# Hashed attention and a squared-ReLU block: another way of loading and transposing the first pair of heads

## The chip, the cores and the metric

The kernel runs on one core of a Trainium2 chip. The metric is the device time of one execution in microseconds, as the median of several runs. The engines named here are TensorE (PE in the profile, with its weight loads as PEld), VectorE (DVE), ScalarE (ACT), GpSimd (POOL) and SyncE (SP), which issues DMAs. ACT and POOL issue DMAs as well.

## The reference

Attention in which a query sees only the keys with the same six-bit hash, then a two-layer block with a squared ReLU.

```python
# q, k, v: (4, 8, 768, 64), proj: (64, 6)
q_bits = (np.einsum('bhsd,dk->bhsk', q, proj) > 0).astype(np.int64)
k_bits = (np.einsum('bhsd,dk->bhsk', k, proj) > 0).astype(np.int64)
powers = 2 ** np.arange(n_bits)
q_bucket = np.sum(q_bits * powers, axis=-1)
k_bucket = np.sum(k_bits * powers, axis=-1)
mask = q_bucket[:, :, :, None] == k_bucket[:, :, None, :]
scores = np.where(mask, scale * np.matmul(q, k.transpose(0, 1, 3, 2)), -1000000000.0)
scores = scores - np.max(scores, axis=-1, keepdims=True)
attn = np.exp(scores)
attn = attn / (np.sum(attn, axis=-1, keepdims=True) + 1e-09)
attn_out = np.matmul(attn, v)
x = attn_out.transpose(0, 2, 1, 3).reshape(3072, 512)
h = x @ w_in                       # (512, 2048)
r = np.maximum(h, 0.0)
out = (r * r) @ w_out              # (2048, 512)
```

## The kernel before

**The whole.** The attention part takes the 32 heads as 16 pairs, two heads of 64 features on the 128 partitions, and lasts to about 318 us. The rest of the span is the two-layer block, done in chunks of 1024 tokens with fewer block products than the plain scheme (`product`, line 828, and `hidden_pair`, line 1091). The order of all instructions is written out by hand under `tc.manual_schedule()` (line 656): each engine runs its own instructions in that order and waits where an operand or a buffer is not ready.

**One pair.** The features of queries and keys stand as `feat`, [features of two heads, query or key, 768 tokens]. The scores come in blocks of 128 keys by 384 queries by two heads (`score`, line 439): `products` multiplies bf16 marks of the hash bits (`bits`), whose product is zero for equal hashes and hugely negative otherwise, and adds the fp32 products of the features in the same PSUM buffer. The first block of the first pair (`first_score`, line 448) has them the other way round: first the feature products of both query halves, then the mark products of both. ACT takes the exponential (`weight`, line 434) into a ring of four `e` tiles. `attend` multiplies `e` by the values, and DVE sums the `e` tiles (`add_up`).

**The marks.** `hash_bits` multiplies the projection by `feat`. For pairs 1 to 15, ACT makes signs of it, and POOL's DMAs place them (`signs`, `weigh`, `place_bits`). The first pair goes another way: `first_signs` (line 364) makes the query marks on ACT in four instructions, and `first_keys` (line 400) the key marks of one half c of the keys on DVE, two comparisons (line 409) and one scaling (line 413).

**PSUM.** There are three pools: `turn` has two buffers that all score blocks, hashes and transposed halves take in turn, `spare` has one, and `xo` has one, called `void` ahead of the first pair and taken by the sums over the values (`outs`) later. Each is of two banks.

**The first pair.** `load_first` (line 277) loads queries and keys: for each of the two and for each head one DMA, head 0 on SP's queue, head 1 on ACT's. A partition holds, for each of six blocks t of 128 tokens, the token t * 128 + p: runs of 64 floats, 256 bytes. Then the projection is loaded for both heads. `keep_busy` (line 333) issues products of ones that nobody reads. `first_features(w, r)` (line 314) transposes three blocks of two heads at once, for the queries (w = 0) or the keys (w = 1) and the first or second half of the tokens (r), into a `turn` buffer. ACT copies the queries to `feat`, DVE the keys (lines 326 and 328). With four such halves and two buffers, the third waits for the copy of the first, the fourth for that of the second, and the two buffers of `first_score` for the copies of the two key halves. All later pairs come by `load_pair` (line 291), eight DMAs on SP's queue in runs of 128 bytes, and are transposed by DVE (`features`, line 340).

**The order at the start** (lines 657 to 674): the ones and zeros, the loads of the first pair, eight filler products, the identity on POOL, constants on DVE and POOL, the loads of pair 1, of the first values (`load_values`, line 305) and of two weight pieces, the query halves, two filler products, the first key half, the hash of the queries into `void`, their signs, the hash of the first keys into `spare` and their marks, the second key half. Then, in the loop over pairs, `load_pair(2)`, `first_score` and `first_keys(1, spare("hash"))`, before the other blocks.

Of the kernel before, what the change touches and what calls it, by code (L numbers as in the profile page):

```python
# [8 lines left out]
FP32 = mybir.dt.float32  # L9
BF16 = mybir.dt.bfloat16  # L10
# [24 lines left out]
def kernel(  # L35
# [10 lines left out]
    nc = tc.nc  # L46
    PSUM = bass.MemoryType.PSUM

    B, H, S, D = q.shape
# [3 lines left out]
    P = 128  # L53
    SB = S // P
    HS = S // 2
# [15 lines left out]
    ident = glob.tile([P, P], FP32, name="ident")  # L71
# [19 lines left out]
    p_qk = first.enter_context(tc.tile_pool(name="p_qk", bufs=2))  # L91
# [4 lines left out]
    const = first.enter_context(tc.tile_pool(name="const", bufs=1))  # L96
# [7 lines left out]
    def turn(name):  # L104

        return ps_s.tile([P, 2, 512], FP32, name=name, tag="turn")

    def spare(name):

        return ps_t.tile([P, 2, 512], FP32, name=name, tag="spare")  # L110
# [164 lines left out]
    nat, feat, bits = {}, {}, {}  # L275

    def load_first():

        both = p_qk.tile([P, 2, SB, 2, D], FP32, name="qk_nat")
        for w, src in enumerate((q, k)):  # L280
            t = both[:, w]
            for h, queue in enumerate((nc.sync, nc.scalar)):
                queue.dma_start(
                    out=t[:, :, h], in_=src[0, h].rearrange("(t p) d -> p t d", t=SB)
                )
        nat[0, "qk"] = both
        feat[0] = p_f.tile([P, 2, S], FP32, name="feat")
        for h, queue in enumerate((nc.sync, nc.scalar)):
            queue.dma_start(out=projs[h * D:(h + 1) * D, 0:NBITS], in_=proj)
# [15 lines left out]
    def load_values(pr):  # L305
        b, j = divmod(pr, PB)
        t = p_v.tile([P, 2, SB * D], FP32, name="v_nat")
        nc.sync.dma_start(
            out=t.rearrange("p h (t d) -> p (h t) d", d=D),
            in_=v[b, 2 * j:2 * j + 2].rearrange("h (t p) d -> p (h t) d", t=SB),  # L310
        )
        nat[pr, "v_nat"] = t

    def first_features(w, r):

        tp = turn("tp")[:, 0]
        for i in range(SB // 2):
            t = r * (SB // 2) + i
            nc.tensor.transpose(  # L319
                out=tp[:, i * P:(i + 1) * P],  # L320
                in_=nat[0, "qk"][:, w, t].rearrange("p h d -> p (h d)"),
                identity=ident,
            )
        out = feat[0][:, w, r * HS:(r + 1) * HS]
        if w == 0:
            nc.scalar.copy(out=out, in_=tp[:, 0:HS])
        else:
            nc.vector.tensor_copy(out=out, in_=tp[:, 0:HS])  # L328

    busy = const.tile([P, 512], BF16, name="busy")  # L330
    void = ps_o.tile([P, 2, 512], FP32, name="xo")

    def keep_busy(n, w=512):

        for _ in range(n):
            nc.tensor.matmul(
                out=void[:, 0, 0:w], lhsT=busy[:, 0:P], rhs=busy[:, 0:w], start=True, stop=True
            )

    def features(pr):  # L340
# [9 lines left out]
    def hash_bits(pr, banks, ws=(0, 1), cs=(0, 1)):  # L350


        for w in ws:
            hashed[pr, w] = banks
            for c in cs:
                g = 2 * w + c
                for h in range(2):
                    rows = slice(h * D, (h + 1) * D)
                    nc.tensor.matmul(  # L359
                        out=banks[g * NR_B:(g + 1) * NR_B, h, 0:HS], lhsT=projs[rows],  # L360
                        rhs=feat[pr][rows, w, c * HS:(c + 1) * HS], start=True, stop=True,
                    )

    def first_signs(w):

        bits[0, w] = t = all_bits[0][:, w]
        for c in range(2):
            at = slice((2 * w + c) * NR_B, (2 * w + c + 1) * NR_B)
            for h in range(2):
                nc.scalar.activation(  # L370
                    out=t[h * D:h * D + NR_B, c * HS:(c + 1) * HS], in_=hashed[0, w][at, h, 0:HS],
                    func=ACTF.Sign, scale=HUGE, bias=lifts[at],
                )
# [26 lines left out]
    def first_keys(c, banks):  # L400

        if c == 0:
            bits[0, 1] = all_bits[0][:, 1]
        t = bits[0, 1]
        hash_bits(0, banks, (1,), (c,))
        at = slice((2 + c) * NR_B, (3 + c) * NR_B)
        cut = slice(c * HS, (c + 1) * HS)
        for h in range(2):
            nc.vector.tensor_scalar(  # L409
                out=t[h * D:h * D + NR_B, cut], in0=banks[at, h, 0:HS],  # L410
                scalar1=0.0, scalar2=None, op0=ALU.is_gt,
            )
        nc.vector.tensor_scalar(
            out=t[:, cut], in0=t[:, cut], scalar1=spans, scalar2=bases, op0=ALU.mult,
            op1=ALU.add,
        )
# [204 lines left out]
    for pr in range(NIN, NP):  # L621
        n = 16 if pr == NP - 1 else 1 + (pr % 3 == 0)
# [13 lines left out]
    def order(n):  # L636

        s = n % NR
        return s if n < NR else s % 2 * NQ + s // 2
# [14 lines left out]
        minus(*((t1, b12, b11), (t2, b22, t1), (t3, b22, b12), (b12, b21, t2))[n - 1])  # L654

    with tc.manual_schedule():
        nc.vector.memset(busy, 1.0)
        nc.vector.memset(projs, 0.0)
        load_first()
        keep_busy(8)  # L660
        make_identity(nc, ident)
        constants()
        load_pair(1)
        load_values(0)
        for i in range(2):
            load_weight(i)
        first_features(0, 0)
        first_features(0, 1)
        keep_busy(2)
        first_features(1, 0)  # L670
        hash_bits(0, void, (0,))
        first_signs(0)
        first_keys(0, spare("hash"))
        first_features(1, 1)


# [1 line left out]
        for pr in range(NP):  # L678
# [86 lines left out]
            if more:  # L765
                load_values(pr + 1)
# [28 lines left out]
        pr = NP - 1  # L795
# [626 lines left out]
        for i in range(NCHUNK):  # L1422
            for s in range(NR):
                r = order(i * NR + s)
# [245 lines left out]
```

## Time and profile before

| What | us |
|---|---|
| median of 3 runs | 858.05 (857.92 to 859.75) |
| the profiled execution | 858.97 |
| its span | 857.2 |
| TensorE busy up to 12.51 us | 8.95 |
| TensorE busy from 12.51 to 857.20 | 839.20 |
| DVE busy up to 12.51, from there | 4.17, 745.11 |
| ACT busy up to 12.51, from there | 4.43, 397.60 |

The span is the stretch that the profiler records; the time of the execution is 1.8 us longer. At 12.51 us the first mark products of the first pair begin (line 429, `st` from `bits`). Busy times of matmuls have modelled ends, so neighbouring ones overlap, and a busy TensorE need not be at its peak. In the chain of waits, each step is followed back to what released it.

### The profile page before, as it was taken

Reading aid. Unit: us, or ns where it says so; the run is one execution under the profiler, and the core shown is the slowest. Engines: PE = TensorE matmul, PEld = TensorE weight load, DVE = VectorE, ACT = ScalarE, POOL = GpSimd, SP = SyncE. Lnnn points to the kernel's source line nnn. Section 1 sums busy time; section 2 is a strip of 40 time slices with the busy share of each in tenths; the row PEclk is TensorE's granted clock in tenths of the full one; section 3 lists DMA queues with packets and bytes.
Section 4 is the critical chain, followed back from the end, with each engine's and each line's share of the span. In section 5 each row is a group of like instructions: output and inputs, shape, how many; then the busy total and the mean of one; then the engine's idle time right before and its main releaser. Section 6 shows DMA issues by size and latency. Waiting matters only on the chain.

```text
span 857.2 us, 16996 instructions
## 1 busy us (share of the span) xinstructions
PE 848.1 (99%) x6593; PEld 529.0 (62%) x6593; DVE 749.3 (87%) x1026; ACT 402.0 (47%) x752; POOL 166.6 (19%) x280
## 2 busy tenths in 40 slices
PE   8999999999999999999999999999999999999997
PEld 3544444444444544444788875657888765668886
DVE  5899999999999988998879978888889788889776
ACT  5887777788877762222211145554111355541110
POOL 1221111113321101653122121111000311100002
PEclk9999999999999999999999999999999999999999
DMA  9676899889998525999976976437557865335466
GB/s 204 133 143 153 176 183 196 201 161 260 247 227 227 169 69 215 342 308 296 355 235 227 264 184 218 163 114 277 196 153 195 179 239 176 124 120 154 149 168 140
DMA packets 236132, 170.12 MB, mean 198 GB/s; under 512 B 169576, under 2 KB 193200, under 8 KB 236048
## 3 DMA queue, kind: packets, MB, share of 16 engines
q1 hardware_dynamic: 195376, 87.85, 41.4%
q0 software_dynamic: 16480, 42.41, 15.9%
q10 hardware_dynamic: 24192, 38.74, 14.7%
q8 instruction: 53, 0.87, 0.4%
q14 instruction: 31, 0.25, 0.1%
HBM read 127.14 MB, written 41.16 MB: 196 GB/s over the span
## 4 chain that ended last, share of the span: by engine, by line
PE 97%; DMA 1%; DVE 0%; POOL 0%; ACT 0%; issue 0%; ACTq 0%; DVEq 0%
PE acc L837 41%; PE st L429 18%; PE xo L484 14%; PE acc L1099 13%; PE acc L1052 8%; PE tot L533 2%; PE hash L359 1%; DMA qk_nat<-in_k_dram 1%; DMA bits<-signed 1%; POOL bits L395 0%; DVE bits L409 0%; PE xo L359 0%; ACT e L435 0%; DVE feat L328 0%; PE tp L319 0%
## 5 line engine op out<-in xcount | busy, mean ns | idle before, releaser
L435 ACT ACTIVATE e<-st 128x768 f32<-128x768 f32 x192 | 155.4, 810 | 59.2 <-PE st L429 56.2
L429 PE MATMUL st<-feat 64*64 64x384 f32 x1536 | 158.0, 483 | 1.0 <-DVE feat L328 1.0
L484 PE MATMUL xo<-e,v_nat 64*64 64x385 f32 (+1 forms) x1520 | 157.6, 483 | 0.0
L837 PE MATMUL acc<-b,leaf 128*128 128x256 f32 x600 | 133.3, 379 | 0.4 <-issue 0.4
L837 PEld LDWEIGHTS acc<-b,leaf 128*128 128x128 f32 x600 | 113.8, 190 | 16.8 <-issue 1.3
L472 DVE TENSOR_TENSOR total<-total,e 128x1536 f32<-128x1536 f32 x64 | 111.8, 1746 | 4.3 <-ACT e L435 2.8
L395 POOL DMA_DIRECT2D bits<-signed x120 | 61.9, 520 | 217.2 <-ACT signed L384 198.4
L484 PEld LDWEIGHTS xo<-e,v_nat 64*64 64x64 f32 (+1 forms) x1520 | 57.3, 133 | 66.4 <-issue 57.8
L1099 PE MATMUL acc<-t_x,w_unit 128*128 128x512 f32 x192 | 90.9, 595 | 0.0
L429 PEld LDWEIGHTS st<-feat 64*64 64x64 f32 x1536 | 56.3, 133 | 38.7 <-issue 33.3
L837 PE MATMUL acc<-t,leaf 128*128 128x256 f32 x336 | 76.0, 379 | 0.0
L837 PEld LDWEIGHTS acc<-t,leaf 128*128 128x128 f32 x336 | 63.8, 190 | 8.7
L914 DVE SCALAR_TENSOR_TENSOR b<-h 128x512 f32<-128x512 f32 x96 | 65.7, 691 | 3.0
L429 PE MATMUL st<-bits 64*64 64x384 bf16 x768 | 65.9, 325 | 0.3
L837 PE MATMUL acc<-x,w_unit 128*128 128x512 f32 x128 | 56.5, 593 | 0.0
L837 PE MATMUL acc<-b_t,leaf 128*128 128x256 f32 x240 | 53.8, 379 | 0.0
L844 ACT COPY two<-acc 128x256 f32<-128x256 f32 (+1 forms) x29 | 12.5, 432 | 87.5 <-PE acc L837 72.1
L1099 PEld LDWEIGHTS acc<-t_x,w_unit 128*128 128x128 f32 x192 | 35.8, 190 | 26.7 <-issue 23.0
L1220 POOL DMA_DIRECT2D out_dram<-h x24 | 15.5, 654 | 182.1 <-DVE h L1215 182.1
L844 ACT COPY one<-acc 128x256 f32<-128x256 f32 (+1 forms) x29 | 12.5, 432 | 78.8 <-PE acc L837 63.7
L837 PEld LDWEIGHTS acc<-b_t,leaf 128*128 128x128 f32 x240 | 45.6, 190 | 6.2
L429 PEld LDWEIGHTS <-bits 64*64 64x64 bf16 x768 | 24.2, 107 | 38.1 <-issue 37.5
(178 smaller groups left out, 1287.9 us busy)
## 6 DMA issues: line engine op xcount, KB each, us to landing
leaf<-w_out ACTq DMA_DIRECT2D x142, 256.0 KB, 3.0
raw<-in_moe_w_in_dram SPq DMA_DIRECT2D x8, 1024.0 KB, 6.7
raw<-in_moe_w_out_dram SPq DMA_DIRECT2D x8, 1024.0 KB, 7.9
w_unit<-w_in SPq DMA_DIRECT2D x16, 512.0 KB, 4.0
w_unit<-w_in SPq DMA_DIRECT2D x8, 896.0 KB, 8.4
w_out<-sums POOLq DMA_DIRECT2D x16, 448.0 KB, 7.6
v_nat<-in_v_dram SPq DMA_DIRECT2D x16, 384.0 KB, 5.2
x_all<-x_t SPq DMA_DIRECT2D x16, 384.0 KB, 3.2
```

The lines of the kernel that those rows point to most:

```text
L395: nc.gpsimd.dma_start(out=t[h * D:h * D + NBITS + 1, w, c * HS:(c + 1) * HS], in_=signed[at:at + NBITS + 1, h],)
L429: nc.tensor.matmul(out=st[k * HK:(k + 1) * HK, h, 0:HS], lhsT=src[1][rows, key], rhs=src[0][rows, cut], start=first, stop=not first, skip_ ...
L435: nc.scalar.activation(out=key_of(pr, kt)[:, :, i, 0:HS], in_=st[:, :, 0:HS], func=ACTF.Exp, scale=scale)
L472: nc.vector.tensor_tensor(out=totals[pr], in0=totals[pr], in1=e, op=ALU.add)
L484: return nc.tensor.matmul(out=outs[pr][h * D:(h + 1) * D, c, 0:HS + 1], lhsT=nat[pr, "v_nat"][rows, h, kt * D:(kt + 1) * D], rhs=key_of(pr ...
L533: done = nc.tensor.matmul(out=spares[pr][g * 32:(g + 1) * 32, c2, 0:QS], lhsT=ones[rows], rhs=totals[pr][rows, h, c, c2 * QS:(c2 + 1) * QS ...
L837: nc.tensor.matmul(out=acc[to], lhsT=a(i), rhs=b(i), start=first and i == 0, stop=last and i == n - 1, skip_group_check=True,)
L844: nc.scalar.copy(out=t, in_=acc[of])
L914: nc.vector.scalar_tensor_tensor(out=out, in0=h, scalar=0.0, in1=h, op0=ALU.max, op1=ALU.mult)
L1052: nc.tensor.matmul(out=out, lhsT=w(a), rhs=b, start=start, stop=stop, skip_group_check=True)
L1099: nc.tensor.matmul(out=to, lhsT=w[:, PLACE[a], f], rhs=bt[b](f), start=first and f == 0, stop=last and f == NFT // 2 - 1, skip_group_check ...
L1220: queue.dma_start(out=out[at, m0 + a * 32:m0 + (a + 1) * 32].rearrange("(c i) j -> i c j", i=32), in_=ot[a * 32:(a + 1) * 32].rearrange("i ...
```

## The change

It touches the first pair alone.

- `load_first`: a partition now holds six consecutive tokens of each head, p * 6 + t, so a run is 384 floats, 1536 bytes. The tile is [partition, query or key, head, t, feature].
- `first_features`: for each block t, one product per head of the loaded [128 tokens, 64 features] with the identity, an ordinary fp32 matmul, instead of one transpose of both heads. The column x of block t is then token x * 6 + t. For the queries, ACT's copy writes every sixth element and so restores the order of the tokens. For the keys, DVE's copy leaves the order as it is. The second key half goes into the `spare` buffer, the others into `turn`.
- `load_values`: the first pair's values are loaded in the same order as the keys, six consecutive tokens to a partition, in runs of 1536 bytes.
- The hash of the first keys goes into `void`. That of the later keys stays in `spare`.
- `keep_busy`: six filler products instead of eight, and the two after the query halves are gone. Their ones are a tile of 128 columns that is read four times over, filled by POOL instead of DVE.

```diff
@@ -276,12 +276,12 @@
 
     def load_first():
 
-        both = p_qk.tile([P, 2, SB, 2, D], FP32, name="qk_nat")
+        both = p_qk.tile([P, 2, 2, SB, D], FP32, name="qk_nat")
         for w, src in enumerate((q, k)):
-            t = both[:, w]
             for h, queue in enumerate((nc.sync, nc.scalar)):
                 queue.dma_start(
-                    out=t[:, :, h], in_=src[0, h].rearrange("(t p) d -> p t d", t=SB)
+                    out=both[:, w, h].rearrange("p t d -> p (t d)"),
+                    in_=src[0, h].rearrange("(p t) d -> p (t d)", t=SB),
                 )
         nat[0, "qk"] = both
         feat[0] = p_f.tile([P, 2, S], FP32, name="feat")
@@ -305,36 +305,44 @@
     def load_values(pr):
         b, j = divmod(pr, PB)
         t = p_v.tile([P, 2, SB * D], FP32, name="v_nat")
-        nc.sync.dma_start(
-            out=t.rearrange("p h (t d) -> p (h t) d", d=D),
-            in_=v[b, 2 * j:2 * j + 2].rearrange("h (t p) d -> p (h t) d", t=SB),
-        )
+        vs = v[b, 2 * j:2 * j + 2]
+        if pr == 0:
+            nc.sync.dma_start(out=t, in_=vs.rearrange("h (p t) d -> p h (t d)", t=SB))
+        else:
+            nc.sync.dma_start(
+                out=t.rearrange("p h (t d) -> p (h t) d", d=D),
+                in_=vs.rearrange("h (t p) d -> p (h t) d", t=SB),
+            )
         nat[pr, "v_nat"] = t
 
     def first_features(w, r):
 
-        tp = turn("tp")[:, 0]
+        tp = (spare("tp") if (w, r) == (1, 1) else turn("tp"))[:, 0]
+        ts = slice(r * (SB // 2), (r + 1) * (SB // 2))
         for i in range(SB // 2):
-            t = r * (SB // 2) + i
-            nc.tensor.transpose(
-                out=tp[:, i * P:(i + 1) * P],
-                in_=nat[0, "qk"][:, w, t].rearrange("p h d -> p (h d)"),
-                identity=ident,
+            for h in range(2):
+                nc.tensor.matmul(
+                    out=tp[h * D:(h + 1) * D, i * P:(i + 1) * P],
+                    lhsT=nat[0, "qk"][:, w, h, ts.start + i], rhs=ident, start=True, stop=True,
+                )
+        if w == 0:
+            nc.scalar.copy(
+                out=feat[0][:, w].rearrange("p (x t) -> p t x", t=SB)[:, ts],
+                in_=tp[:, 0:HS].rearrange("p (t x) -> p t x", x=P),
             )
-        out = feat[0][:, w, r * HS:(r + 1) * HS]
-        if w == 0:
-            nc.scalar.copy(out=out, in_=tp[:, 0:HS])
         else:
-            nc.vector.tensor_copy(out=out, in_=tp[:, 0:HS])
-
-    busy = const.tile([P, 512], BF16, name="busy")
+            nc.vector.tensor_copy(out=feat[0][:, w, r * HS:(r + 1) * HS], in_=tp[:, 0:HS])
+
+    busy = const.tile([P, P], BF16, name="busy")
     void = ps_o.tile([P, 2, 512], FP32, name="xo")
 
-    def keep_busy(n, w=512):
-
+    def keep_busy(n):
+
+        wide = busy.rearrange("p (o n) -> p o n", o=1).to_broadcast([P, 4, P])
         for _ in range(n):
             nc.tensor.matmul(
-                out=void[:, 0, 0:w], lhsT=busy[:, 0:P], rhs=busy[:, 0:w], start=True, stop=True
+                out=void[:, 0].rearrange("p (o n) -> p o n", o=4), lhsT=busy, rhs=wide,
+                start=True, stop=True,
             )
 
     def features(pr):
@@ -654,10 +662,10 @@
         minus(*((t1, b12, b11), (t2, b22, t1), (t3, b22, b12), (b12, b21, t2))[n - 1])
 
     with tc.manual_schedule():
-        nc.vector.memset(busy, 1.0)
+        nc.gpsimd.memset(busy, 1.0)
         nc.vector.memset(projs, 0.0)
         load_first()
-        keep_busy(8)
+        keep_busy(6)
         make_identity(nc, ident)
         constants()
         load_pair(1)
@@ -666,11 +674,10 @@
             load_weight(i)
         first_features(0, 0)
         first_features(0, 1)
-        keep_busy(2)
         first_features(1, 0)
         hash_bits(0, void, (0,))
         first_signs(0)
-        first_keys(0, spare("hash"))
+        first_keys(0, void)
         first_features(1, 1)
```

## The prediction

> **What bounds the kernel now.** I read the page first. TensorE is busy for 99% of the span, and its granted clock is 9 tenths or more in all 40 slices.
>
> ```profile
> PE 848.1 (99%) x6593; PEld 529.0 (62%) x6593; DVE 749.3 (87%) x1026; ACT 402.0 (47%) x752; POOL 166.6 (19%) x280
> PEclk9999999999999999999999999999999999999999
> ```
>
> So 857.2 - 848.1 = 9.1 us of TensorE idleness is in the whole span, and an edit that removes no needed product gains only by starting the dense stream sooner. Busy time split at 12.51 us shows 8.95 us of TensorE work before that point, 3.6 of the idle 9.1 us, and much of the 8.95 is filler (L336). After it DVE is busy 745.1 of 844.7 us and TensorE 839.2, so TensorE stays the pace. The next view is the chain of waits of the first 45 us (start, length, what).
>
> ```profile
> 1.51 5.90 DMA qk_nat<-in_k_dram
> 7.50 0.52 PE tp L319 x3
> 8.02 0.86 PE xo L359 x8
> 8.88 0.65 PE hash L359 x4
> 9.63 0.55 DVE bits L409
> 10.20 0.57 DVE bits L409
> 10.79 0.38 DVE bits L413
> 11.20 0.57 DVE feat L328
> 11.81 1.20 PE st L429 x16
> ```
>
> The reader sees one serial thread: the keys of head 1 land at 7.41, are transposed, the queries and then the first keys are hashed, DVE makes the key marks, and only then copies the second half of the keys out of PSUM (L328, 11.20 to 11.77). TensorE stands until that copy, because the second score buffer is the one being copied. The score stream's mark products begin at 12.51, and from there TensorE hardly stops. I use 12.51 as the mark to be moved. The timeline from 0 to 12 us shows what is ahead.
>
> ```profile
> 1.69 3.60 PE L336 MATMUL xo<-busy 128*128 128x512 bf16 x8 [1.69 <-DVE excess L255]
> 2.09 0.15 PEld L336 LDWEIGHTS <-busy 128*128 128x128 bf16 x1 [0.28 <-issue]
> 2.52 0.15 PEld L336 LDWEIGHTS <-busy 128*128 128x128 bf16 x1 [0.28 <-issue]
> 5.18 1.04 PE L319 MATMUL tp<-ident,qk_nat 128*128 128x128 f32 x6
> 8.99 2.36 ACT L370 ACTIVATE bits<-xo,lifts 32x384 bf16<-32x384 f32 x4 [2.21 <-issue]
> ```
>
> Filler products are 0.43 us apart (512 columns), about half the speed of the later stream, where 256 columns in two-pass fp32 take 0.222 us (L837: 133.3 us / 600). The first transpose took 448 ns, the others 272. So the array speeds up at about 5.2 us, which the granted clock does not show.
>
> The DMA view from 0 to 3 us gives the landings (last number, us after issue began): q at 0.97 + 3.6 = 4.6 and 0.98 + 4.1 = 5.1, k at 1.48 + 4.8 = 6.3 and 7.4, the projection at 7.8 and 8.0.
>
> ```profile
> qk_nat<-in_q_dram SPq DMA_DIRECT2D x1, 192.0 KB, 3.6
> qk_nat<-in_q_dram ACTq DMA_DIRECT2D x1, 192.0 KB, 4.1
> qk_nat<-in_k_dram SPq DMA_DIRECT2D x1, 192.0 KB, 4.8
> qk_nat<-in_k_dram ACTq DMA_DIRECT2D x1, 192.0 KB, 5.9
> projs<-in_proj_dram ACTq DMA_DIRECT2D x1, 1.5 KB, 5.8
> ```
>
> **The loads.** The four loads are 3072 runs of 256 bytes and become 512 of 1536. With both queues active, 3.5 to 4.0 us moved 575 packets at 285 GB/s with the 16 engines full; the 4 KB runs of the weights (14 to 18 us) reach 401 GB/s. No row has 1536 bytes; the ends are 285 and 401, and I take 350, between them. First bytes move at 2.1 us in either kernel. q: 393 KB / 350 = 1.1 us, and the last packet came about 0.8 us before the semaphore (4.3 against 5.1), so 2.1 + 1.1 + 0.8 = 4.0. k: 1.1 later, plus 0.3 for pair 1's 128-byte runs, which start on SP's queue behind it: 5.4. The projection, 0.6 behind k as on ACT's queue now, about 5.9. The ends are q 3.7 to 4.8 and k 4.9 to 6.6. Pair 1's loads (SP held from 2.71 to 6.78 on four of them) and the first values, 1536 runs made 256, move up with them, by 2 us or so: both are needed only after the mark (15.37 and 15.05), so this only keeps them ahead of a stream that comes sooner.
>
> **The products that transpose.** Three transposes per half become six fp32 products, which the trace counts as two instructions each (L429's 768 own products stand there as 1536): 12 of 128 columns. The nearest row is K=128, M=64 in the last values (L484, 128*64): 8 of 385 columns in 1.52 us, so the two column halves run beside each other, at about 0.16 us each; scaled to 128 columns 0.053. Twelve give 0.64 us as the lower end. Weight loads cost 0.136 each if nothing hides them: 12 x (0.136 + 0.053) = 2.3 us as the upper end. In the dense stream 12 loads of 64 columns go through in 0.81 us, 0.067 each: I take 12 x 0.067 = 0.8 us per half, plus 0.2 until the result can be read. Now it is 3 x 0.14 + 0.27 = 0.55 in all (0.52 seen).
>
> [...]
>
> **The copies.** ACT's copy of 128x384 takes 0.48; it now writes every sixth element. No row writes so: between 0.48 and twice that, I take 0.48, since no row shows a price for an output's step. DVE's copy stays 0.56.
>
> **PSUM and filler.** `spare` for the second key half takes DVE's L328 off the way to the second score buffer; instead the hash of the later keys waits for that copy, and its rows (`first_keys(1)`) are queued behind the marks. The filler's ones are written by POOL (128x1536 takes 1.37 us there, so 128x128 about 0.11) ahead of the identity, which moves from 1.54 to about 1.7 and is needed at 4.0; POOL's clearing of the bits ends near 4.3, read after 7. DVE's constants come 0.48 earlier, nobody waits. The filler runs from 1.2 to 1.2 + 6 x 0.43 = 3.8. The two dropped later fillers lay in a wait for k and cost nothing.
>
> **The sum.** q 4.05; first half issued by 4.85, read by ACT 5.05 to 5.55; second half to 5.65, copied by 6.35. First key half needs k (5.4) and the first buffer (5.55): 5.65 to 6.45, copied by DVE 6.65 to 7.25. Hash of q from 6.5 (0.93), ACT's signs 7.45 to 9.8 (2.36). Hash of the first keys 7.25 to 8.1 (0.84), DVE 1.12 + 0.38 to 9.7. Meanwhile TensorE: second key half to 8.75, both sets of own products 2 x 0.65 to 10.05. Mark products at 10.1 against 12.51: 2.4 sooner. Given back: the hash of the later keys comes 0.43 after the marks now (12.94), and will wait for the L328 copy (9.75 to 10.3, seen at 10.4) and the buffer behind it, about 0.2. Net **-2.2 us**. The profiled execution is 858.97 us with span 857.2, so 855.0 of span and 856.8 in all; the median shown is 0.92 below that execution, so **855.85**. With the best ends (q 3.7, 0.64 per half) marks come at about 9.1, -3.2.
>
> **Rivals.** (B) The start is no sooner, only the wait moves: loads bound by something else than run length, or copies at double price. With q and k landing as now: 5.15, halves to 6.85, key half 7.45 to 8.3, copy 9.05, hash 9.95, marks 11.6, net -0.7: 857.35. For it: engines were full already at 285 GB/s, completions trail by up to 1.6 us. Against: 401 GB/s in the same trace.
>
> (C) Slower: the array stays at its slow rate. It sped up 3.5 us after the first filler, in an unbroken run; now the filler lasts 2.6 us and a hole follows until q. If it waits for the next unbroken stretch, halves take 1.6, hashes double: marks near 13.5 (+1.0), then some 1.4 us at half rate (+0.7): 859.75. It decides if the speed-up comes later than about 10 us; before that a gain remains. Against: idle stretches of 0.8 and 1.0 us did not slow the array again in this trace, and the hole is 0.3. [...]
>
> (D) Slower: weight loads unhidden. 2.3 per half puts the key half's copy at 11.6 and the marks at 14.3, +1.8: 859.85. The L484 row speaks against it. [...]
>
> (E) The longer runs don't come about, or later waits take up all: 858.05.
>
> **How the numbers follow.** Forecast 58%, B 22%, E 5%, C 10%, D 5%. A measurement of this kernel tells some 0.2% (1.7 us) from no change. The forecast case (-1.7 to -3.4) is faster: 58%. B and E are within: 27%. C and D are slower: 15%. The range: 854.3 leaves out the best tail, 859.0 leaves out most of C and D. The likeliest case's own range is 854.6 to 856.4.
>
> **What would show it.** Right: q's first product near 4.0 to 4.3, k landed by 5.5, 12 instructions per half in 0.8 to 1.0 us, first st<-bits near 10.1, no wait of st on L328, the rest of the span unchanged in length (844.7 us after the mark). Wrong: transposing instructions twice as long after 5.2 us (C), weight loads in series (D), landings at 5.1 and 7.4 (B), or idle TensorE time after the mark that grows by as much as the start shrank.

## The result and the profile after

The changed kernel takes 860.42 us (median of 22 runs, 859.59 to 861.63), the kernel before 859.22 beside it (22 runs, 857.64 to 863.01): ratio 1.0018, 95% interval 1.0011 to 1.0024. The forecast was 2.2 us faster; it is 1 to 2 us slower, and outside the range.

Page of the changed kernel, part 1, and its DMA view from 0 to 3 us (the last number of a DMA line is us from the start of its issue to its landing):

```profile
PE 849.6 (99%) x6625; PEld 529.5 (62%) x6625; DVE 749.0 (87%) x1025; ACT 402.8 (47%) x752; POOL 167.3 (19%) x281
```

```profile
qk_nat<-in_q_dram SPq DMA_DIRECT2D x1, 192.0 KB, 3.2
qk_nat<-in_q_dram ACTq DMA_DIRECT2D x1, 192.0 KB, 3.4
qk_nat<-in_k_dram ACTq DMA_DIRECT2D x1, 192.0 KB, 4.2
qk_nat<-in_k_dram SPq DMA_DIRECT2D x1, 192.0 KB, 3.8
...
projs<-in_proj_dram SPq DMA_DIRECT2D x1, 1.5 KB, 4.4
projs<-in_proj_dram ACTq DMA_DIRECT2D x1, 1.5 KB, 4.2
```

The loads did what they were said to do. With the starts of issue (0.98 for both q, 1.43 for both k, 1.90 and 1.92 for the projection) the queries are there at 4.4, the keys at 5.6 instead of 7.4, the projection at 6.3 instead of 8.0. From 3 to 4.5 us the DMAs move 392 GB/s, where runs of 256 bytes had 285 (3.5 to 4.0 us).

The chain of waits of the changed kernel (start, length, what), to be read beside that of the kernel before, which the prediction shows:

```profile
6.48 0.88 PE tp L324 x12
7.35 0.82 PE xo L367 x8
...
8.26 0.57 ACT bits L378
...
10.01 0.58 ACT bits L378
10.59 0.04 issue
10.63 0.83 PE xo L367 x4
11.47 1.12 PE tp L324 x12
12.59 3.09 PE st L437 x24
```

Before, the chain went from the hash of the queries straight to the hash of the first keys. Now ACT's four signs (L378) lie between: the hash of the first keys, into `void`, starts at 10.63, right behind the last sign, though its keys were copied by 7.96 and TensorE was free at 8.18. The table of windows shows TensorE in that stretch and after it (first number behind the window is its length, then busy time and count of each engine, then the granted clock, the DMA share and GB/s):

```profile
8.18:10.63 2.45, 0.00 (x0) 0.00 (x0) 0.00 (x0) 2.29 (x4) 0.00 (x0) 1.00 1.42 155
11.80:15.20 3.40, 3.40 (x30) 1.44 (x30) 1.87 (x4) 0.00 (x0) 0.00 (x0) 0.50 1.00 402
```

First 2.45 us without one product, with ACT alone at work; then 3.4 us in which TensorE has work all the time at a granted clock of 0.50. The trace's record of the clock has this stretch from 11.81 to 15.22, 3.41 us. That record begins only when the clock is first full, here at 4.98: up to there the products that transpose start every 0.11 us on average, from there every 0.055. I call that the rise of the clock. The timeline shows the wait, and what the halved clock does to the score products:

```profile
8.26 2.33 ACT L378 ACTIVATE bits<-xo,lifts 32x384 bf16<-32x384 f32 x4 [1.14 <-PE xo L367]
10.63 0.83 PE L367 MATMUL xo<-feat,projs 64*32 64x384 f32 x4 [2.50 <-ACT bits L378]
...
12.52 2.84 PE L437 MATMUL st<-feat 64*64 64x384 f32 x16
15.14 0.55 PE L437 MATMUL st<-bits 64*64 64x384 bf16 x8
```

Sixteen products in 2.84 us; the same sixteen take 1.52 in the runs below. The first mark products come at 15.14. In the kernel before they come at 12.51, 2.63 sooner:

```profile
12.51 0.51 PE L429 MATMUL st<-bits 64*64 64x384 bf16 x8
```

When ACT first copies sums over the values out of PSUM (`x_raw`, 36.94 against 34.68), 2.26 of that is left: the profile before has a wait for pair 1's bits at 28.12 (four mark products in 0.79 us) that this one doesn't have. At the end the spans differ by 1.4 (858.6 and 857.2). Single executions spread over 2.0 us for the changed kernel and 5.4 for the one before, so I read the start from the traces and the whole from medians.

The length of the slow stretch, 3.41 us, is a step that comes back in the record of the clock: from the rise to the fall it is 6.83 us, two steps, and from 15.22 to the next fall, at the end of the span (858.32), 843.09 us, 247 steps. Where an expectation below speaks of a window of the clock, it means such a step. In the step ahead of the slow stretch, 8.40 to 11.81, TensorE was without a product for 2.23 us; how much idle time went with a fall is worked out from the traces below, where the changed kernel is run again.

### The profile page after: what moved, and what is told of

It is laid out like the page before. It is cut to its first block, busy times and chain, and to the rows that moved or that the text cites. A ratio compares the mean times of both kernels' runs of the same rounds, so it can differ in the third digit from the quotient of the medians.

```text
span 858.6 us, 17062 instructions
## 1 busy us (share of the span) xinstructions
PE 849.6 (99%) x6625; PEld 529.5 (62%) x6625; DVE 749.0 (87%) x1025; ACT 402.8 (47%) x752; POOL 167.3 (19%) x281
## 4 chain that ended last, share of the span: by engine, by line
PE 97%; DVE 1%; ACT 0%; DMA 0%; POOL 0%; issue 0%; ACTq 0%; DVEq 0%; POOLq 0%
PE acc L844 39%; PE st L437 19%; PE xo L492 15%; PE acc L1106 13%; PE acc L1059 8%; PE tot L541 2%; PE hash L367 1%; DMA out_dram<-h 0%; PE tp L324 0%; DVE o L1208 0%; DVE h L1222 0%; POOL bits L269 0%; ACT bits L378 0%; PE xo L367 0%; DVE tmp L1208 0%
```

## The experiments

Theory W: the loss is a wait, made by sharing one buffer between the hash that ACT still reads and the hash that TensorE is to write, and what the standstill does to the clock. All runs have the kernel before beside them on the same chip. The table sums up: first mark products, first `x_raw` copy (both in the profile) and the ratio of the times to those of the kernel before in its set.

| kernel | marks, us | `x_raw`, us | ratio, 95% interval |
|---|---|---|---|
| before | 12.51 | 34.68 | 1 |
| changed | 15.14 | 36.94 | 1.0018 (1.0011 to 1.0024) |
| changed, again | 14.30 | 36.05 | 1.0020 (1.0011 to 1.0030) |
| hash in a turn buffer | 11.44 | 33.20 | 0.9981 (0.9973 to 0.9990) |
| hash written ahead of the signs | 11.40 to 13.10 | 34.67 | 1.0008 (0.9999 to 1.0016) |
| fillers in the wait | 13.30 | 35.06 | 1.0032 (1.0021 to 1.0044) |
| before, hash in `void` | 15.37 | 37.72 | 1.0048 (1.0036 to 1.0060) |
| loads only | 12.27 | 34.02 | 0.9988 (0.9978 to 0.9998) |
| before, PSUM part only | 11.58 | 33.33 | 0.9986 (0.9977 to 0.9995) |
| turn buffer, plain copy | 10.52 | 32.27 | 0.9973 (0.9962 to 0.9983) |
| turn buffer, old fillers | 11.18 | 32.93 | 0.9988 (0.9978 to 0.9998) |
| turn buffer, DVE copies half | 10.97, 11.18 | 32.73, 32.93 | 0.9979 (0.9969 to 0.9988), 0.9983 (0.9973 to 0.9993) |

**The hash in another buffer.** One word changed, against the changed kernel:

```diff
-        first_keys(0, void)
+        first_keys(0, turn("hash"))
```

> Theory W: the hash of the first keys stands in the buffer whose query half ACT's signs still read, and waits for them (2.45 us from 8.18 to 10.63); that standstill then halves the array's clock from 11.8 to 15.2 us. With the hash in a turn buffer the wait is gone: hash at 8.2, first mark products near 10.9 (15.14 in the changed kernel, 12.51 before), no stretch of granted clock 0.50 before 20 us, time 1 to 2 us under the kernel before. Rival R1 (the wait only shows another lateness, copies or marks): mark products not before 14, time like the changed kernel, 1.2 over. Rival R2 (the clock falls because of the thin start with fewer fillers, not because of the wait): the 0.50 stretch stays, marks near 12.5, time like the kernel before.

It came as theory W has it: 1.5 us under the kernel before (856.73 and 858.25). Its timeline, TensorE first, then ACT and DVE:

```profile
7.80 0.85 PE L367 MATMUL xo<-feat,projs 64*32 64x384 f32 x8
8.53 0.84 PE L367 MATMUL hash<-feat,projs 64*32 64x384 f32 x4
9.30 0.88 PE L324 MATMUL tp<-ident,qk_nat 128*64 128x128 f32 x12
10.10 1.52 PE L437 MATMUL st<-feat 64*64 64x384 f32 x16
11.44 0.50 PE L437 MATMUL st<-bits 64*64 64x384 bf16 x8
...
8.77 2.37 ACT L378 ACTIVATE bits<-xo,lifts 32x384 bf16<-32x384 f32 x4 [1.02 <-PE xo L367]
...
9.49 1.12 DVE L417 TENSOR_SCALAR bits<-hash 32x384 bf16<-32x384 f32 x2 [1.02 <-PE hash L367]
```

The hash of the first keys (8.53) follows that of the queries without a hole, while ACT's signs run from 8.77 to 11.14, and from 6.2 us on the clock stays full. DVE reads its hash beside ACT's signs.

**The order of writing.** The same instructions in the same order on each engine, with the same buffers; only which of two waits for the other is turned round:

```diff
-        first_signs(0)
         first_keys(0, void)
+        first_signs(0)
```

> Same instructions in the same order on every engine, same buffers; only written so that the hash of the first keys comes before the signs, which turns the wait round: ACT then waits for the hash. Theory W: hash at 8.2, ACT's signs start near 9.05 instead of 8.26 and end near 11.4, first mark products 11.2 to 11.5, no 0.50 stretch, time 0.5 to 1.3 us under the kernel before. R1: mark products not before 14. R2: 0.50 stretch stays and time like the kernel before or over it.

The wait changed sides, and more than I thought of it. ACT's signs waited not only for the hash of the keys but for DVE's reading of it:

```profile
9.45 1.12 DVE L417 TENSOR_SCALAR bits<-xo 32x384 bf16<-32x384 f32 x2 [1.02 <-PE xo L367]
10.69 2.36 ACT L378 ACTIVATE bits<-xo,lifts 32x384 bf16<-32x384 f32 x4 [3.10 <-DVE bits L417]
13.10 0.35 PE L437 MATMUL st<-bits 64*64 64x384 bf16 x3 [0.28 <-ACT bits L378]
```

DVE reads partitions 64 to 95, ACT 0 to 63, and neither writes there; still ACT starts when DVE has ended its two readings of `xo` (10.57), and it doesn't wait for the scaling that DVE does next. With the hash in another buffer, above, the two ran side by side (DVE from 9.49 to 10.61, ACT from 8.77 to 11.14). So in these two kernels uses of one PSUM tile by different engines stood in line in the order of writing, though they touched different partitions: the products from 10.63, behind the last sign (10.59), in the changed kernel, the signs from 10.69, behind DVE's readings (10.57), here. The mark products trickle in behind the signs until 13.10, and the time is that of the kernel before, within the noise: the forecast of 0.5 to 1.3 us under missed. Whether this wait is needed is not shown: no run here lets the two go at once on one tile.

**Fillers in the wait.** The wait stays, eleven filler products into the idle spare buffer keep TensorE busy:

```diff
         first_signs(0)
+        fill = spare("fill")
+        for _ in range(11):
+            nc.tensor.matmul(
+                out=fill[:, 0].rearrange("p (o n) -> p o n", o=4), lhsT=busy,
+                rhs=busy.rearrange("p (o n) -> p o n", o=1).to_broadcast([P, 4, P]),
+                start=True, stop=True,
+            )
         first_keys(0, void)
```

> The wait stays, but 11 filler products into the idle spare buffer run in it. Theory W: hash of the first keys still at 10.6, but clock 1.00 throughout, mark products near 13.5 (1.6 sooner than in the changed kernel), time 1.2 to 1.7 under the changed kernel, that is 0 to 0.5 us under the kernel before. If the clock's fall cost nothing (DVE's marks set the pace anyway, rival R1): marks near 15, time like the changed kernel. R2: the 0.50 stretch stays at the same place or a window later.

In the trace it is what theory W expects:

```profile
10.39 0.84 PE L367 MATMUL xo<-feat,projs 64*32 64x384 f32 x4
...
13.30 0.51 PE L437 MATMUL st<-bits 64*64 64x384 bf16 x8
```

The hash comes at 10.39, the marks 2.91 later (4.51 in the changed kernel, where 10.63 led to 15.14), so the halved clock cost 1.6 us there. The same windows as above:

```profile
8.18:10.63 2.45, 2.43 (x13) 0.92 (x12) 0.00 (x0) 2.12 (x4) 0.00 (x0) 1.00 1.43 147
11.80:15.20 3.40, 3.40 (x46) 1.41 (x41) 2.19 (x6) 1.51 (x2) 0.00 (x0) 1.00 1.01 405
```

The time does not follow: 861.11, ratio 1.0032, where 0 to 0.5 us under the kernel before was expected. Part of it is outside the span: time less span is 3.3 us here in the median and 1.6 to 1.8 in every other kernel, for a reason I haven't found. By spans the kernel is 1.1 us over the one before (857.75 and 856.65), where the changed kernel, in the next set, was 2.05 over (858.85 and 856.8).

**The shared buffer alone.** The kernel before with this one part of the change:

```diff
-        first_keys(0, spare("hash"))
+        first_keys(0, void)
```

> The kernel before with this one part of the change: the hash of the first keys in the buffer that the signs read. Theory W: that hash waits from 8.88 to the end of the signs at 11.35, DVE's marks and the L328 copy follow 2.5 later, mark products near 15.0 instead of 12.51; with a fall of the clock behind it up to 16.5; time 2 to 3.5 us over the kernel before. R1: the buffer makes no difference, within 0.3 us of the kernel before.

The old loads have the same hole, and the wait on L328 besides:

```profile
9.12 2.33 ACT L370 ACTIVATE bits<-xo,lifts 32x384 bf16<-32x384 f32 x4 [1.64 <-PE xo L359]
11.50 0.84 PE L359 MATMUL xo<-feat,projs 64*32 64x384 f32 x4 [2.49 <-ACT bits L370]
14.67 0.88 PE L429 MATMUL st<-feat 64*64 64x384 f32 x8 [1.05 <-DVE feat L328]
```

The mark products come at 15.37, 2.86 later than before, and the kernel is slower by 0.36% to 0.60%, some 3 to 5 us: more than expected. The clock did not fall in this profile, though the hole is as long (2.49). In 4 of the 6 executions the mean clock is 0.998 or less, but the profiled one, at 1.000, took 862.47 too, so the clock alone does not explain the excess over the forecast, and its cause stays open. A standstill of 2.5 us was thus followed by a halved clock in one profile (the changed kernel, 2.45 us) and not in another (this one, 2.49).

**The changed kernel again.**

> The changed kernel as it is, once more, beside the others of this set. Theory W (wait of 2.45 us, then the halved clock): about 1.2 to 1.6 us over the kernel before, hash of the first keys again starting when the last of the signs ends. If the 0.50 stretch depends on how the start falls against the clock's windows, it may be absent or elsewhere in this profile; then the mark products come near 13.5 instead of 15.1.

The second case came up: full clock from 6.90 on, marks at 14.30 (13.5 expected).

```profile
11.39 0.83 PE L367 MATMUL xo<-feat,projs 64*32 64x384 f32 x4 [2.50 <-ACT bits L378]
...
14.30 0.51 PE L437 MATMUL st<-bits 64*64 64x384 bf16 x8
```

The hash waited 2.50 us for the signs again, from a later start, and from the hash to the marks it is 2.91 us, as with the fillers. That bears out the 1.6 us for the halved clock.

Why did the clock fall in one profile and not in the other? Count steps of 3.41 us from the rise (4.98 in the first profile, 6.90 here). In the first, the hole put 2.23 idle us into one step, 8.40 to 11.81. Here it is split at 10.31, some 1.4 before and 1.1 after (TensorE stands from 8.89 to 11.39), and in the kernel before with the hash in `void`, split at 10.36, some 1.4 and 1.1 as well. The ends of the spans, where TensorE runs out of work, test this further: the clock falls there in all thirteen profiles. All fourteen falls lie a whole number of such steps behind the rise (in the kernel before 249: 849.92 us from 5.59). The step ahead of a fall had 2.23 us or more without a product, and no step with 1.7 or less was followed by a fall. The nearest cases on each side, as windows (length, then TensorE's busy time): the step ahead of the fall in the changed kernel, and the last step ahead of the fall at the end with the hash in a turn buffer; then the step from 6.90 in the second profile, and a step near the end of the kernel with the loads only, described next, both without a fall behind them:

```profile
8.40:11.81 3.41, 1.18 (x12) 0.55 (x14) 0.18 (x1) 2.15 (x4) 0.00 (x0) 1.00 1.31 220
849.33:852.74 3.41, 0.81 (x4) 0.20 (x2) 0.76 (x3) 0.27 (x1) 0.00 (x0) 1.00 0.56 103
...
6.90:10.31 3.41, 1.72 (x23) 0.78 (x20) 0.56 (x1) 2.11 (x4) 0.00 (x0) 1.00 1.41 148
849.62:853.03 3.41, 1.77 (x9) 1.03 (x7) 1.65 (x5) 0.27 (x1) 0.00 (x0) 1.00 0.43 71
```

So in these traces a fall went with the idle time within one step, 2.23 us or more, and 1.7 us or less went without one; how a hole falls against the steps decides which it is. In 19 of the 34 executions of the changed kernel the mean clock is 0.998 or less, in 8 of 88 of the kernel before in the sets that list it (the halved clock at the end of a span lowers this mean too: 1.71 us at 0.50 in the profile before, by 0.001). The clock's part in the loss is therefore a matter of chance for each execution, and I give no figure for it in the median.

**The other parts.** With both PSUM moves undone, the loads, the products that transpose and the dropped fillers are left:

```diff
-        first_keys(0, void)
+        first_keys(0, spare("hash"))
-        tp = (spare("tp") if (w, r) == (1, 1) else turn("tp"))[:, 0]
+        tp = turn("tp")[:, 0]
```

> The changed kernel with both PSUM moves undone: second key half in a turn buffer, hash of the first keys in the spare one. Left are the long runs, the products that transpose, the strided copy and the fewer fillers. Theory W: no wait for the signs; hash of the first keys near 8.3, DVE's marks to 10.7, the L328 copy (now L334) to 11.3, mark products near 12.0 to 12.3; time 0 to 0.8 us under the kernel before. Rival R3 (loads and products are worth the whole loss of the changed kernel): mark products at 13 or later, time 1 us over.

```profile
11.57 0.88 PE L437 MATMUL st<-feat 64*64 64x384 f32 x8 [0.69 <-DVE feat L334]
12.27 0.51 PE L437 MATMUL st<-bits 64*64 64x384 bf16 x8
```

The old wait on the second key half's copy is back (0.69 us), and the gain is 0.24 us in the marks, 0.02% to 0.22% in time. And the PSUM part on the old loads, with the hash in a turn buffer:

```diff
-        tp = turn("tp")[:, 0]
+        tp = (spare("tp") if (w, r) == (1, 1) else turn("tp"))[:, 0]
-        first_keys(0, spare("hash"))
+        first_keys(0, turn("hash"))
```

> The kernel before (old loads, transposes and fillers) with only the PSUM part, done so that nothing waits for the signs: second key half in the spare buffer, hash of the first keys in a turn buffer. Theory W: the wait on L328 is gone, mark products near 11.4 to 11.7 instead of 12.51, time 0.7 to 1.1 us under the kernel before. Rival R4 (that wait was hidden by signs and marks anyway): mark products at 12.2 or later, within 0.3 us of the kernel before.

```profile
11.58 0.51 PE L429 MATMUL st<-bits 64*64 64x384 bf16 x8
```

Marks at 11.58, as expected, with no wait between the two sets of own products. The two parts are worth 0.12% and 0.14% singly and 0.19% together in the turn-buffer run, which the intervals allow to be a sum.

**The strided copy.** On the turn buffer, ACT copies as the columns stand:

```diff
-                out=feat[0][:, w].rearrange("p (x t) -> p t x", t=SB)[:, ts],
-                in_=tp[:, 0:HS].rearrange("p (t x) -> p t x", x=P),
+                out=feat[0][:, w, r * HS:(r + 1) * HS], in_=tp[:, 0:HS],
```

> Hash of the first keys in a turn buffer, and ACT copies the first pair's queries as they stand in PSUM, without restoring the order of the tokens (the outputs of the first pair's queries are therefore in another order). It isolates the price of writing every sixth element: copies of 0.48 instead of 0.86 us; if the strided write is on the path, mark products 0.4 to 0.7 us sooner than with the turn buffer alone (10.7 to 11.0) and time 1.9 to 2.3 us under the kernel before; if not, 1.5 under.

By groups of instructions, first the turn buffer as it is, then with the plain copy (busy, mean ns of one):

```profile
L329 ACT COPY feat<-tp 128x384 f32<-128x384 f32 x2 | 1.7, 846 | 2.3 <-PE tp L324 2.3
```

```profile
L329 ACT COPY feat<-tp 128x384 f32<-128x384 f32 x2 | 1.0, 479 | 1.9 <-PE tp L324 1.9
```

Writing every sixth element costs 0.37 us a copy. The marks come 0.9 sooner, at 10.52, and the time is 2.1 us under the kernel before (856.26 and 858.40); a part of that is the clock, which rose at 4.7 here and at 6.2 in the other profile.

**The old fillers.** On the turn buffer, eight fillers and two again:

```diff
-        keep_busy(6)
+        keep_busy(8)
         first_features(0, 1)
+        keep_busy(2)
```

> Hash of the first keys in a turn buffer, with the old number of fillers (8 and 2). If the dropped fillers cost nothing (theory W): within 0.4 us of the turn buffer alone, 1.2 to 1.7 us under the kernel before; the eight end near 4.8 and push the first product by 0.3. If the fewer fillers delay the full clock (rival R2): full clock by 5.2 in this kernel and time 2 us or more under the kernel before.

Within the noise of the turn buffer alone. The full clock came at 4.6; with six fillers it came between 4.1 and 6.9 in nine profiles, in the three profiles with the start of the kernel before (eight fillers, from 1.69 us on) at 5.0, 5.6 and 6.95. These profiles show no effect of the number of fillers.

**A version that beats both.** On the turn buffer, DVE copies the second query half, so that the strided copies run beside each other:

```diff
-            nc.scalar.copy(
+            (nc.vector.tensor_copy if r else nc.scalar.copy)(
```

> Hash of the first keys in a turn buffer, and DVE instead of ACT copies the second query half, so that the two strided copies (0.86 us each on ACT) run beside each other. If the strided copies are on the path: hash of the queries 0.3 to 0.5 sooner, mark products near 11.0 (11.44 with the turn buffer alone), time 1.7 to 2.2 us under the kernel before. If DVE pays more for the stride or the landing of k sets the pace: like the turn buffer alone, 1.5 under.

> The turn buffer with DVE copying the second query half, once more, to see whether it beats both kernels again: 1.5 to 2 us under the kernel before, mark products near 11.

856.70 against 858.40, and 857.54 against 858.69: faster than the kernel before both times, and like the turn buffer alone within the intervals. DVE's strided copy takes 0.85 us, as ACT's does, where its plain one takes 0.56.

## Why the prediction was wrong

**The step that failed** is in the sum: "Hash of the first keys 7.25 to 8.1 (0.84)", beside "ACT's signs 7.45 to 9.8". Both use `void`, and I let them run at once; the paragraph on PSUM priced the move of the second key half and passed over the hash's new buffer. The diff and the order by hand had it: `first_signs(0)` reads `void`, `first_keys(0, void)` stands behind it. The runs put 2.45 us in that place, and one word changed, another buffer for that hash, turned 1 to 2 us of loss into 1.5 us of gain.

**From there the rest of the sum.** Marks were forecast at 10.1 and came at 15.14. Of the 5.04 us, 0.93 had gone before the hash could start (8.18 for 7.25), 2.45 are the wait, 1.66 lie behind it, which the halved clock explains (1.6 by the run with fillers and by the second profile).

**The 0.93** had mostly built up when the first buffer came free, at 6.44 instead of 5.55. The first product started 0.28 later than forecast (4.33 for 4.05). The first half took 1.26 up to ACT's copy instead of 1.0, with the clock full only from 4.98 on. The copy took 0.85 instead of 0.50, the upper end that I named and did not take. That "no row shows a price for an output's step" was a poor reason for the lower end: the runs show one, 0.37 us on 384 elements at a step of 24 bytes, and no run here tries another step. Without the wait and without the stride (turn buffer, plain copy, clock full from 4.7 on) the marks came at 10.52, 0.4 behind the forecast: the rest of the sum was near.

**Right:** the landings, nearly (q 4.0 forecast, 4.4 seen; k 5.4 and 5.6; projection 5.9 and 6.3), though not by the rate that I took: it was 392 GB/s, not 350, and they still came later. The products that transpose: at full clock 12 in 0.88 us (0.8 plus 0.2 forecast), so rival D fell: in those 0.88 us the products are busy for 0.87 and the weight loads for 0.63, so the loads went on beside the products, with all 128 rows in use. The L484 row had spoken for it: in series its eight loads (0.136 us each) and products (0.16, an estimate from that row) would take 2.4 us, and 1.52 were seen. The L328 wait is gone with the spare buffer, as said. After the mark the rest kept its length to within 1.2 us (858.6 - 15.14 = 843.5 against 844.7).

**The rivals.** C named the clock and missed its cause: the fewer fillers did not delay the rise, a standstill that I had not seen made it fall. The half rate that C reckons with is in the runs: fillers start 0.43 us apart ahead of the rise, and eleven at full clock take 2.55 us, 0.23 each (fillers in the wait). That "idle stretches of 0.8 and 1.0 us did not slow the array again" held; 2.45 us did, in one of two profiles of the changed kernel. The tables of the granted clock do not show the first rise, as I said, but they show the fall; the record begins at the rise, 5.59 in the kernel before, where I read 5.2 (the transposes there take 448, 358 and then 273 ns). B and E don't describe the runs: the start was late, with a new wait in it. I gave 15% to slower, and none of it to this wait.

## What to carry to other kernels

When a tile moves to another PSUM buffer, list who still uses that buffer at that point in the written order; in this program partitions that don't overlap did not help, and even two readers on two engines stood in line (ACT from 10.69, DVE to 10.57). On an engine that is the bound, a hole can have a second price: here one of 2.45 us was followed by 3.41 us of full work at clock 0.50, in the profile where 2.23 us of it fell into one step of 3.41 us. An order restored in the copy is paid for in the copy, 0.37 us on top of 0.48 at a step of six fp32.

## What was not expected of the hardware

The clock's rise at the start came anywhere from 4.1 to 6.9 us after the start of the span in nine profiles whose fillers began at the same 1.23 us, so early TensorE work differs between executions of one kernel (in the two profiles of the changed kernel the rise is at 4.98 and 6.90, the hash of the queries at 7.29 and 8.04). A hole of 2.45 to 2.50 us was followed by 3.41 us at clock 0.50 in one of three profiles, the one in which 2.23 us of it lay in one step. And eleven products more in the prologue came with 1.6 us more outside the span (3.3 against 1.7), unexplained.
